# Four half-loaded projections and a new order: a transformer layer on one core

## The chip, the cores and the metric

The kernel runs on one core of a Trainium2 chip. The metric is device time in microseconds (us) of one execution; the median of three runs of the kernel before is 200.46 us (199.8 to 200.73).

## The reference

One layer over 2048 positions of width 512, in bf16: a normalised input goes through a sliding-window attention with 32 heads of 16 (each position sees 8 positions, two apart), the result is added back, normalised again, and goes through a gated feed-forward part of inner width 1376 (1376 = 10 x 128 + 96).

```
h   = x + A(layernorm(x))
  A:  q, k, v = x @ wqkv                          # 512 x 1536
      logits  = q . k[pos - 2*w], w = 0..7, / 4   # masked where pos - 2*w < 0
      o       = softmax(logits) . v[pos - 2*w];  o @ wo
h2  = h + ((relu(hn @ W_gate)) * (hn @ W_up)) @ W_down,  hn = layernorm(h)
```

## The kernel before

The 2048 positions are cut into four chunks of 512 (`tk` 0 to 3; the text writes a step of chunk 2 as `mu1.2`). Everything stays on the chip between load and store. Per chunk the steps are, with the names that the code gives them and the engine that runs them:

- `xst`, `xag` (VectorE statistics), `xrl`, `xre` (ScalarE), `xxn` (VectorE: a normalised row block of 128 positions), then the transpose of the block: on TensorE with an eviction by ScalarE (`xtp` and `xte`; in chunk 0 blocks 1 and 3 are evicted by VectorE, `xtv1`, `xtv3`), or, for all of chunk 3, by four DMA transposes on the SP queue (`xtd`, line 484).
- `qkv0` to `qkv11`: twelve projections of 128 columns (q and k in turn, then four of v), each four TensorE matmuls over the four row pieces of 128 of the weight; ScalarE evicts them (`qe`, line 544). In chunk 0 the first four are cut into halves of 256 positions, `qka0` to `qka3` for the first half and `qkc0` to `qkc3` for the second (lines 547 to 553), so that a half can start when its two row blocks are there.
- `pr1`, `pr0` (VectorE, line 583): products of q with the shifted k, four of 2.2 us per chunk; `sc1`, `sc0` (TensorE, line 589) sum them over each head; `ex` (ScalarE) exponentials; `mk` a mask in chunk 0; `den`, `dl`, `dr` the reciprocal of the denominator; `am` (VectorE) scales the exponentials.
- `bc1`, `bc0` spread the exponentials over a head's partitions (TensorE, evicted as `be`), in chunks 2 and 3 by DMAs on SP (`bd`, line 679). `mu0` to `mu3` (VectorE, line 710) multiply by the shifted v; `tree` sums the eight products. The first addition of a `tree` is in chunks 0 to 2 a DMA that accumulates, `ta` (POOL queue, line 742, 512 KB each).
- `wo0` to `wo3` (TensorE), `rs` (residual), `hnm`, `hsq`, `hrl`, `hre`, `hxn`: second normalisation; its transposes are `htp` and `hte` (TensorE, ScalarE) or DMA transposes `htd` on SP.
- `mm0` to `mm5` (up and gate), `ue`, `ge` (ScalarE), `gu` (VectorE), `dn` (down), `o` (VectorE), `os` (store, on SP but for the last).

The order is fixed at build time. Each step is an `Op` with an engine, a modelled duration and its dependencies; `RANK` gives one number to each of 722 steps, and `Plan.order` (line 116) lets every engine's queue take its own steps in the order of these numbers. Model times only decide in which of several equal buffers a step's result is put. On the chip each engine runs its queue in order, and a step that waits holds up all that stands behind it. The loads are issued ahead of this in `setup` (line 288): four row blocks of x, then the q and k weights in four row pieces of 128 rows, pieces 0 and 2 on the SP queue, 1 and 3 on ACT's (lines 293 and 294), then the second chunk of x and the rest. The planner knows the q and k weights as two loads that land together (`wload["q"]`, `wload["k"]`). `wv_sb` and all later weights follow on SP.

In the first 60 us TensorE takes the projections of all four chunks as filler between the steps that wait for VectorE; then the feed-forward matmuls do that.

The functions that the change touches:

Of the kernel before, what the change touches and what calls it, by code (L numbers as in the profile page):

```python
# [8 lines left out]
P = 128  # L9
# [9 lines left out]
    0, 1, 2, 3, 4, 5, 6, 7, 8, 9, 10, 11, 12, 13, 14, 15, 16, 18, 19, 21,  # L19
    24, 32, 27, 17, 20, 22, 25, 26, 30, 35, 36, 29, 34, 37, 39, 41, 43, 47, 23, 28,  # L20
    31, 33, 38, 45, 48, 42, 59, 65, 40, 51, 55, 46, 56, 60, 49, 52, 57, 73, 76, 61,
    79, 67, 72, 71, 74, 80, 106, 88, 95, 75, 96, 91, 104, 103, 93, 113, 119, 127, 70, 85,
    94, 98, 102, 172, 175, 185, 130, 134, 136, 149, 152, 105, 108, 110, 114, 111, 188, 197, 223, 226,
    231, 179, 190, 217, 221, 228, 171, 180, 208, 211, 219, 158, 169, 195, 207, 210, 245, 252, 236, 241,
    239, 244, 243, 249, 256, 260, 247, 253, 246, 250, 255, 261, 266, 269, 276, 281, 275, 279, 285, 278,
    283, 282, 286, 291, 310, 315, 326, 330, 293, 322, 314, 324, 348, 329, 361, 337, 345, 339, 342, 346,
    350, 365, 333, 358, 349, 354, 340, 352, 353, 356, 363, 323, 328, 316, 321, 302, 313, 308, 312, 332,
    364, 373, 366, 370, 306, 379, 369, 394, 405, 359, 393, 355, 380, 402, 404, 421, 442, 445, 395, 424,
    453, 574, 374, 413, 447, 450, 389, 409, 436, 473, 50, 53, 44, 62, 54, 64, 58, 63, 66, 69,
    77, 90, 78, 83, 92, 81, 87, 82, 86, 89, 118, 129, 157, 170, 124, 196, 164, 178, 97, 101,  # L30
    166, 182, 100, 116, 150, 159, 132, 186, 107, 176, 137, 156, 109, 126, 200, 213, 218, 237, 232, 240,
    251, 258, 262, 264, 274, 284, 287, 288, 296, 294, 292, 298, 300, 307, 305, 309, 303, 318, 327, 360,
    367, 311, 319, 341, 347, 336, 343, 372, 377, 325, 334, 368, 375, 382, 385, 384, 388, 381, 383, 386,
    398, 390, 392, 397, 400, 387, 396, 401, 403, 406, 407, 408, 411, 414, 417, 410, 418, 412, 419, 422,
    457, 467, 434, 484, 477, 480, 461, 481, 491, 472, 475, 429, 466, 449, 460, 441, 476, 478, 433, 435,
    454, 458, 446, 451, 439, 443, 462, 474, 503, 427, 431, 469, 486, 502, 505, 508, 493, 512, 465, 525,
    507, 518, 511, 521, 529, 497, 516, 504, 513, 520, 531, 552, 569, 572, 524, 541, 666, 707, 514, 533,
    537, 540, 536, 539, 580, 708, 112, 120, 99, 121, 68, 84, 115, 122, 125, 133, 144, 163, 147, 160,
    165, 142, 148, 135, 145, 161, 229, 234, 233, 242, 187, 202, 177, 199, 174, 183, 192, 194, 184, 189,
    206, 235, 212, 215, 181, 191, 193, 205, 214, 238, 289, 265, 297, 317, 248, 257, 290, 301, 331, 335,  # L40
    338, 357, 344, 362, 371, 415, 425, 456, 459, 423, 432, 464, 470, 430, 438, 468, 471, 391, 399, 448,
    455, 479, 483, 490, 495, 485, 492, 482, 488, 487, 489, 499, 501, 494, 496, 498, 506, 509, 515, 519,
    522, 526, 528, 527, 534, 517, 532, 596, 601, 562, 594, 565, 589, 558, 591, 604, 544, 553, 542, 551,
    555, 560, 548, 550, 570, 549, 557, 546, 556, 579, 583, 568, 573, 586, 599, 608, 609, 614, 571, 576,
    603, 611, 618, 617, 626, 613, 629, 588, 631, 606, 627, 632, 620, 624, 585, 616, 635, 639, 662, 668,
    672, 623, 641, 643, 677, 628, 636, 638, 675, 634, 637, 645, 647, 117, 141, 128, 139, 131, 140, 123,
    138, 143, 146, 155, 162, 153, 167, 168, 173, 151, 154, 204, 225, 254, 268, 273, 299, 259, 270, 209,
    227, 216, 220, 267, 280, 224, 230, 201, 222, 198, 203, 263, 272, 271, 277, 304, 295, 320, 376, 378,
    351, 416, 420, 426, 428, 437, 444, 440, 463, 452, 530, 535, 543, 561, 500, 510, 523, 566, 547, 554,
    564, 567, 538, 545, 559, 563, 593, 597, 575, 578, 577, 581, 582, 587, 600, 602, 590, 598, 584, 595,  # L50
    592, 605, 607, 610, 619, 622, 615, 625, 621, 633, 612, 630, 657, 689, 683, 687, 667, 673, 671, 680,
    692, 640, 656, 658, 660, 648, 654, 650, 661, 664, 676, 679, 644, 652, 678, 682, 655, 663, 684, 649,
    651, 653, 670, 642, 646, 665, 669, 674, 694, 696, 685, 693, 659, 690, 681, 686, 698, 691, 699, 688,
    697, 701, 710, 714, 717, 719, 705, 709, 711, 715, 695, 702, 704, 706, 700, 703, 712, 713, 716, 718,
    720, 721,
# [36 lines left out]
class Plan:  # L92
# [23 lines left out]
    def order(self):  # L116
# [14 lines left out]
        while left:  # L131
# [36 lines left out]
            op.start, op.done = t, t + op.dur + op.lat  # L168
            if op.dq:
                at = max(t + op.dur + op.dq[0], free.get("DQ", 0.0)) + op.dq[1]  # L170
                free["DQ"] = at
                op.done = at + op.lat
            free[op.eng] = t + op.dur
# [18 lines left out]
def kernel(  # L192
# [19 lines left out]
    DIL = 2  # L212
# [3 lines left out]
    PRE = ()  # L216
    NAB = 0
# [127 lines left out]
    DAL = 5.5  # L345
    TDD, TDL = 1.25, 1.5
# [13 lines left out]
    HG = ([[0, 1, 2, 3]],) * 4  # L360

# [12 lines left out]
    def load(t):  # L374
        return add(None, "LD", 0.0, None, lat=t)

    xload = [[load(t) for t in (3.5, 3.7, 4.1, 4.35)]] + [[load(t)] * BPC for t in (9.15, 13.2, 15.4)]
    wload = {n: load(t) for n, t in
             (("q", 7.78), ("k", 7.78), ("v", 10.6), ("o", 17.1), ("u", 20.5), ("g", 24.0), ("d", 28.5))}
# [139 lines left out]
    for tk in range(NCK):  # L519
# [10 lines left out]
        for n, (c, t) in enumerate(seq):  # L530
# [3 lines left out]
            def f_mm(lo=0, hi=CS, c=c, t=t, mm=mm, xnT=xnT):  # L534
                for dt in range(NT):
                    nc.tensor.matmul(mm.t[:, lo:hi], lhsT=wv_sb[:, dt, t:D:NT] if c == 2 else wqk_sb[:, dt, c * D + t:(c + 1) * D:NT],  # L536
                                     rhs=xnT.t[:, dt, lo:hi], start=(dt == 0), stop=(dt == NT - 1))
# [9 lines left out]
            if tk == 0 and n < 4:  # L547

                a = None
                for i, (lo, hi, evs) in enumerate(((0, 2 * P, xev[0:2]), (2 * P, CS, xev[2:]))):  # L550
                    a = add(("qk%s%d" % ("ac"[i], n), tk), "PE", 4 * MM * (hi - lo) / CS + 0.02,
                            lambda f=f_mm, lo=lo, hi=hi: f(lo, hi), evs + [wl, a, fills[-1]], pr - 5, take=[mm],
                            use=[xnT], lat=PEL if i == 1 else 0.0)
            else:
                a = add(("qkv%d" % n, tk), "PE", 4 * MM, f_mm, xev + [wl], pr, take=[mm], use=[xnT], lat=PEL)
# [13 lines left out]
        for hf in range(2):  # L569
            sc, ex = Buf(at_s), Buf(ex_s)  # L570
            scd, prd = [], []
            for t in range(0, NT, 2):
# [13 lines left out]
                def f_sc(t=t, sc=sc, pb=pb):  # L586
                    for u in range(2):
# [5 lines left out]
                a = add(("pr%d" % hf, tk), "DVE", D40, f_pr, [d[k] for k in (t, t + 1) for d in (qd, kd, kp)],  # L593
                        apr, take=[pb], use=[qT], lat=DL)
                prd.append((a, pb, f_sc))
            if (tk, hf) in PRE:
# [72 lines left out]
        for w0 in range(0, W, BCN):  # L669
            hf = w0 // 4  # L670
            if (tk, hf) in BCD:
                for eng, q in (("SP", nc.sync), ("ACT", nc.scalar), ("POOL", nc.gpsimd)):
# [4 lines left out]
                    def f_bd(ws=ws, q=q, w0=w0, ab=ab, ex=exs[hf]):  # L677
                        for w in ws:
# [3 lines left out]
                                   take=[ab], use=[exs[hf]], lat=0.77, dq=(0.75 - 0.5 * (len(ws) - 1), 0.5 * len(ws))))  # L682
# [19 lines left out]
        for t in range(NT):  # L702
# [13 lines left out]
            def f_om(t=t, mt=mt, rc=rc, OT=OT):  # L716
                V.tensor_tensor(out=OT.t[:, t, :], in0=mt.t[:, 0, :], in1=rc.t[:], op=ALU.mult)

            m = add(("mu%d" % t, tk), "DVE", D40, f_mu, abd + [vd[t], kdone.get(("v", tk - 1, t))], tpr,
                    take=[mt], use=[ab], lat=DL)  # L720
# [17 lines left out]
            for n, du in ((4, D20), (2, D10), (1, D2)):  # L738
                f = lambda n=n, mt=mt, f=f_a: f(n, mt)
                if n == 4 and (tk, t) in DACC:  # L740
                    def f_da(mt=mt):
                        nc.gpsimd.dma_start(mt.t[:, 0:4, :], mt.t[:, 4:8, :], accum_op=ALU.add)  # L742

                    m = add(("ta%d" % t, tk), "POOL", 1.0, f_da, [m], tpr, use=[mt], lat=1.1, dq=(0.75, 2.74))
                    continue
                if n == 1 and tk in EARLY:
                    oev[t] = add(("tree%d" % t, tk), "DVE", du, f_al, [m], tpr, take=[OT], use=[mt], lat=DL)
                else:
                    m = add(("tree%d" % t, tk), "DVE", du, f, [m], tpr, use=[mt], lat=0.11)
# [39 lines left out]
        for f0 in range(0, NFT, 2):  # L789
# [3 lines left out]
            for ft in fts:  # L793
# [4 lines left out]
                def f_mm(w_sb, mm, ft=ft, fs=fs, hnT=hnT):  # L798
                    for dt in range(NT):
                        nc.tensor.matmul(mm.t[:fs, :], lhsT=w_sb[:, dt, ft * P: ft * P + fs],  # L800
                                         rhs=hnT.t[:, dt, :], start=(dt == 0), stop=(dt == NT - 1))
# [4 lines left out]
                def f_ge(gm=gm, gr=gr, fs=fs, i=ft - f0):  # L806
                    nc.scalar.activation(out=gr.t[:fs, i, :], in_=gm.t[:fs, :], func=ACT.Relu)  # L807

                a = add(("mm%d" % (f0 // 2), tk), "PE", 4 * MM, lambda f=f_mm, um=um: f(wu_sb, um), hev + [wload["u"]], pr,
                        take=[um], use=[hnT], lat=PEL)  # L810
                b = add(("ue%d" % (f0 // 2), tk), "ACT", A5, f_ue, [a], pr - 200, take=[ub], use=[um], lat=AL)
                c = add(("mm%d" % (f0 // 2), tk), "PE", 4 * MM, lambda f=f_mm, gm=gm: f(wg_sb, gm), hev + [wload["g"]], pr,
                        take=[gm], use=[hnT], lat=PEL)
# [93 lines left out]
```

## Time and profile before

| | |
|---|---|
| median of three runs | 200.46 us (199.8 to 200.73) |
| the profiled execution, its own time | 201.23 us |
| its span in the trace | 199.5 us |
| TensorE (PE) busy | 191.6 us, 96% |
| VectorE (DVE) / ScalarE (ACT) busy | 152.6 us, 77% / 115.0 us, 58% |
| granted TensorE clock | 1.00 in every stretch asked for |

The profiled execution is 1.73 us longer than its span, and 0.8 us longer than the median of the runs; a difference in the trace is therefore taken off the median. Rows of a timeline give start, duration, engine, line and operation, what is written and read, how many instructions were merged, and in brackets how long the engine was idle before and what ended that. Matmul durations overlap, because matmuls are pipelined: the pace is read from the distance of starts. Four matmuls of 512 positions take 0.86 us in the chain that ended last, a matmul of 256 positions 0.108 us, a transpose 0.055 us.

### The profile page before, as it was taken

Reading aid. Unit: us, or ns where it says so; the run is one execution under the profiler, and the core shown is the slowest. Engines: PE = TensorE matmul, PEld = TensorE weight load, DVE = VectorE, ACT = ScalarE, POOL = GpSimd, SP = SyncE. Lnnn points to the kernel's source line nnn. Section 1 sums busy time; section 2 is a strip of 40 time slices with the busy share of each in tenths; the row PEclk is TensorE's granted clock in tenths of the full one; section 3 lists DMA queues with packets and bytes.
Section 4 is the critical chain, followed back from the end, with each engine's and each line's share of the span. In section 5 each row is a group of like instructions: output and inputs, shape, how many; then the busy total and the mean of one; then the engine's idle time right before and its main releaser. Section 6 shows DMA issues by size and latency. Waiting matters only on the chain.

```text
span 199.5 us, 2918 instructions
## 1 busy us (share of the span) xinstructions
PE 191.6 (96%) x1080; PEld 95.7 (48%) x1099; DVE 152.6 (77%) x239; ACT 115.0 (58%) x240; POOL 12.6 (6%) x28
## 2 busy tenths in 40 slices
PE   8599999999999999999999999999999999999994
PEld 8385445554445344444444444444444444444542
DVE  6669999999999999998899859999964423032332
ACT  3455899881999987663844557701439620456500
POOL 4000000330000004100113000000000000000000
PEclk9999999999999999999999999999999999999999
DMA  6959981897000008985269970140010130102022
GB/s 166 327 185 324 412 283 32 156 192 148 3 0 0 3 0 157 190 165 123 39 118 196 208 204 2 26 85 20 3 53 0 26 79 0 31 0 79 0 79 79
DMA packets 19981, 20.92 MB, mean 105 GB/s; under 512 B 8608, under 2 KB 16768, under 8 KB 19968
## 3 DMA queue, kind: packets, MB, share of 16 engines
q1 hardware_dynamic: 17520, 13.60, 23.0%
q0 software_dynamic: 1728, 6.29, 16.8%
q10 hardware_dynamic: 720, 0.85, 1.6%
q8 instruction: 8, 0.13, 0.3%
q14 instruction: 5, 0.04, 0.1%
HBM read 8.42 MB, written 2.10 MB: 53 GB/s over the span
## 4 chain that ended last, share of the span: by engine, by line
PE 91%; DMA 4%; ACT 2%; issue 1%; SPq 1%; DVE 0%
PE bank L800 37%; PE bank L536 21%; PE bank L837 19%; PE bank L762 7%; DMA wqk_sb<-in_A_wqkv_dram 4%; PE bank L589 3%; PE bank L495 2%; ACT big L695 1%; PE bank L639 1%; ACT quad L511 1%; PE bank L765 0%; SPq L292 0%; PE bank L689 0%; ACT quad L544 0%; SPq L294 0%
## 5 line engine op out<-in xcount | busy, mean ns | idle before, releaser
L800 PE MATMUL bank<-quad,wu_sb 128*128 128x512 bf16 (+1 forms) x170 | 42.7, 379 | 0.7 <-ACT quad L511 0.3
L800 PE MATMUL bank<-quad,wg_sb 128*128 128x512 bf16 (+1 forms) x173 | 41.6, 379 | 0.1
L837 PE MATMUL bank<-wd_sb,gT 128*128 128x512 bf16 (+3 forms) x184 | 39.4, 366 | 0.2
L807 ACT ACTIVATE gr<-bank 128x512 bf16<-128x512 f32 (+1 forms) x44 | 25.3, 601 | 23.3 <-PE bank L800 21.8
L804 ACT CAST up_sb<-bank 128x512 bf16<-128x512 f32 (+1 forms) x44 | 25.1, 588 | 23.2 <-PE bank L800 22.4
L710 DVE TENSOR_TENSOR big<-big,vT 128x4096 bf16<-128x4096 bf16 x16 | 36.1, 2290 | 0.8 <-DMA big<-ex 0.6
L583 DVE TENSOR_TENSOR big<-quad,kT 128x4096 bf16<-128x4096 bf16 x16 | 36.2, 2288 | 0.4 <-ACT quad L544 0.4
L536 PE MATMUL bank<-quad,wqk_sb 128*128 128x512 bf16 (+1 forms) x140 | 30.3, 356 | 2.1 <-DMA wqk_sb<-in_A_wqkv_dram 1.8
L820 DVE TENSOR_TENSOR gT<-gr,up_sb 128x1024 bf16<-128x1024 bf16 (+1 forms) x24 | 15.2, 646 | 20.5 <-ACT up_sb L804 10.4
L837 PEld LDWEIGHTS <-gT 128*128 128x128 bf16 (+1 forms) x187 | 18.2, 98 | 19.7
L800 PEld LDWEIGHTS <-wu_sb 128*128 128x128 bf16 (+1 forms) x176 | 17.5, 100 | 21.1 <-issue 1.3
L800 PEld LDWEIGHTS <-wg_sb 128*128 128x128 bf16 (+1 forms) x176 | 17.6, 100 | 20.5 <-issue 0.2
L536 PEld LDWEIGHTS <-wqk_sb 128*128 128x128 bf16 x144 | 15.5, 114 | 14.3 <-DMA wqk_sb<-in_A_wqkv_dram 2.3
L848 DVE TENSOR_TENSOR row<-x_sm,bank 128x512 bf16<-128x512 bf16 (+1 forms) x17 | 10.8, 653 | 10.6 <-PE bank L837 10.6
L713 DVE TENSOR_TENSOR big<-big 128x1024 bf16<-128x1024 bf16 (+2 forms) x24 | 17.2, 735 | 0.7 <-DMA big<-big 0.6
L742 POOL DMA_DIRECT2D big<-big x12 | 10.5, 872 | 86.8 <-DVE big L710 42.7
L536 PE MATMUL bank<-quad,wv_sb 128*128 128x512 bf16 x62 | 15.2, 380 | 0.1
L762 PE MATMUL bank<-wo_sb,quad 128*128 128x512 bf16 x63 | 15.2, 379 | 0.1
L466 DVE TENSOR_SCALAR row<-x_sm,mv,rs 128x512 bf16<-128x512 bf16 x32 | 11.6, 407 | 2.3 <-ACT rs L448 2.1
L431 DVE BATCH_NORM_STATS2 st<-x_sm 128x6 f32<-128x512 bf16 x16 | 10.5, 680 | 3.4 <-DMA x_sm<-in_A_x_dram 3.4
L420 ACT ACTIVATE row<-x_sm,mv 128x512 bf16<-128x512 bf16 x12 | 8.6, 723 | 5.0 <-DVE mv L412 5.0
L544 ACT CAST kT<-bank 128x512 bf16<-128x512 f32 x16 | 9.2, 592 | 3.4 <-PE bank L536 3.4
(68 smaller groups left out, 141.6 us busy)
## 6 DMA issues: line engine op xcount, KB each, us to landing
big<-big POOLq DMA_DIRECT2D x12, 512.0 KB, 5.5
big<-ex SPq DMA_DIRECT2D x16, 128.0 KB, 2.8
out_dram<-row SPq DMA_DIRECT2D x15, 128.0 KB, 1.8
x_sm<-in_A_x_dram SPq DMA_DIRECT2D x3, 512.0 KB, 6.4
wu_sb<-in_B_W_up_dram SPq DMA_DIRECT2D x1, 1376.0 KB, 9.7
wg_sb<-in_B_W_gate_dram SPq DMA_DIRECT2D x1, 1376.0 KB, 12.7
wd_sb<-in_B_W_down_dram SPq DMA_DIRECT2D x1, 1280.0 KB, 15.7
wqk_sb<-in_A_wqkv_dram ACTq DMA_DIRECT2D x2, 256.0 KB, 7.2
```

The costliest lines, as they stand in the source:

```text
L466: V.tensor_scalar(out=xn.t[:], in0=x, scalar1=mv.t[:, j, 0:1], scalar2=rs.t[:, j:j + 1], op0=ALU.add if residual else ALU.subtract, op1=AL ...
L536: nc.tensor.matmul(mm.t[:, lo:hi], lhsT=wv_sb[:, dt, t:D:NT] if c == 2 else wqk_sb[:, dt, c * D + t:(c + 1) * D:NT], rhs=xnT.t[:, dt, lo:h ...
L583: V.tensor_tensor(out=pb.t[:].rearrange("p (t w) s -> p t w s", t=2), in0=q4, in1=k4, op=ALU.mult)
L710: V.tensor_tensor(out=mt.t[:], in0=ab.t[:], in1=v8, op=ALU.mult)
L713: V.tensor_tensor(out=mt.t[:, 0:n, :], in0=mt.t[:, 0:n, :], in1=mt.t[:, n:2 * n, :], op=ALU.add)
L762: nc.tensor.matmul(od.t[:], lhsT=OT.t[:, t, j * P:(j + 1) * P], rhs=wo_sb[:, t, :], start=(t == 0), stop=(t == NT - 1 and tk not in RPE))
L800: nc.tensor.matmul(mm.t[:fs, :], lhsT=w_sb[:, dt, ft * P: ft * P + fs], rhs=hnT.t[:, dt, :], start=(dt == 0), stop=(dt == NT - 1))
L804: nc.scalar.copy(out=ub.t[:fs, i, :], in_=um.t[:fs, :])
L807: nc.scalar.activation(out=gr.t[:fs, i, :], in_=gm.t[:fs, :], func=ACT.Relu)
L820: V.tensor_tensor(out=gt.t[:fs, 0:n, :], in0=gr.t[:fs, 0:n, :], in1=ub.t[:fs, 0:n, :], op=ALU.mult)
L837: nc.tensor.matmul(od.t[:, c0:c1], lhsT=gts[ft].t[:fs, ft % 2, j * P:(j + 1) * P], rhs=wd_sb[:fs, ft, c0:c1], start=(ft == 0), stop=(ft == ...
L848: V.tensor_tensor(out=ob.t[:, c0:c1], in0=x_sm[:, tk * BPC + j, c0:c1], in1=od.t[:, c0:c1], op=ALU.add)
```

## The change

It has four parts.

1. The first four projections of chunk 0 are cut in three: `qka` and `qkc` are now the two halves of 256 positions over weight row pieces 0 and 1 only, two matmuls each, and a new step `qkd` adds pieces 2 and 3 over all 512 positions, two matmuls. The halves wait for a new planner load `ab` (pieces 0 and 1), `qkd` for the old one. The flag that starts an accumulation is set in the first half only, since both halves now stay open in one PSUM bank until `qkd`.
2. `RANK` is a new list of 727 numbers: four more `qkd` and one more load.
3. The planner's model: later landing times of the loads, and a DMA model in which a transfer from SP or ACT that comes while accumulating DMAs of the POOL queue are under way is slowed (to a share of 0.06 for a DMA transpose, 0.18 for others), and can hold up its queue. This changes planned times, and by them the numbers of the buffers; it issues nothing.
4. Options that are off (`PRD`, `DAC2`, `PRS`, `MUH`, `HSP` are all empty) and the loops that go with them; with them empty the same instructions are issued as before.

```diff
-                for dt in range(NT):
+            def f_mm(lo=0, hi=CS, d0=0, d1=NT, ...):
+                for dt in range(d0, d1):
...
-                                     rhs=xnT.t[:, dt, lo:hi], start=(dt == 0), stop=(dt == NT - 1))
+                                     rhs=xnT.t[:, dt, lo:hi], start=(dt == 0 and lo == 0), stop=(dt == NT - 1))
...
-                a = None
+                ab, done = [wload["ab"]], []
                 for i, (lo, hi, evs) in enumerate(((0, 2 * P, xev[0:2]), (2 * P, CS, xev[2:]))):
-                    a = add(("qk%s%d" % ("ac"[i], n), tk), "PE", 4 * MM * (hi - lo) / CS + 0.02,
-                            lambda f=f_mm, lo=lo, hi=hi: f(lo, hi), evs + [wl, a, fills[-1]], pr - 5, take=[mm],
-                            use=[xnT], lat=PEL if i == 1 else 0.0)
+                    done.append(add(("qk%s%d" % ("ac"[i], n), tk), "PE", 2 * MM * (hi - lo) / CS + 0.005,
+                                    lambda f=f_mm, lo=lo, hi=hi: f(lo, hi, 0, 2), evs + ab + done + [fills[-1]], pr - 5,
+                                    take=[mm], use=[xnT]))
+                a = add(("qkd%d" % n, tk), "PE", 2 * MM, lambda f=f_mm: f(0, CS, 2, NT), done + [wl], pr - 4.9, take=[mm],
+                        use=[xnT], lat=PEL)
...
-    xload = ... for t in (9.15, 13.2, 15.4)]
+    xload = ... for t in (10.8, 14.4, 17.8)]
-             (("q", 7.78), ("k", 7.78), ("v", 10.6), ...
+             (("q", 9.55), ("k", 9.55), ("ab", 8.1), ("v", 12.1), ...
```

The new numbers, set against the list of steps, give the new queues. The places that the prediction speaks of, before and after:

```
TensorE, start
  before: xtp0 xtp1 fill fill | qka1 qka0 xtp2 xtp3 qka2 qka3 | qkc1 qkc3 qkc2 qkc0 | qkv5 qkv6 qkv7 qkv4 qkv10 qkv8
          xtp.1 xtp.1 xtp.1 qkv9 xtp.1 qkv11 | sc1.0
  after:  xtp0 xtp1 fill fill | qka3 qka1 xtp3 xtp2 qka2 qka0 | qkc2 qkc0 qkd0 qkd2 qkc1 qkd1 qkc3 qkd3 |
          qkv6 qkv5 qkv7 qkv4 qkv8 xtp.1 xtp.1 xtp.1 qkv11 xtp.1 qkv10 | sc1.0      (qkv9 stands behind sc0.0 now)
VectorE, start
  before: xxn3 xxn2 | xst.1 xtv3 xst.1 xag xst.1 xst.1 xag xag xag xst.2 | pr1.0 xxn.1 x4 xag.2 pr1.0 pr0.0
  after:  xxn3 xxn2 xtv3 | xst.1 x4 xag.1 x4 | pr1.0 xxn.1 x4 pr1.0 pr0.0           (xst.2 behind pr0.0)
VectorE, chunk 3's rows
  before: xxn.3 xxn.3 xxn.3 mu3.0 xxn.3 mu2.0 mu1.0 mu0.0
  after:  mu3.0 xxn.3 xxn.3 xxn.3 xxn.3 mu2.0 mu1.0 mu0.0
TensorE, before the feed-forward part
  before: ... qkv11.3 qkv2.3 htp.0 x4 bc0.1 sc1.2 mm0.0 sc0.2 bc1.1
  after:  ... qkv11.3 htp.0 x4 qkv9.3 qkv7.3 sc1.2 bc0.1 mm3.0 mm2.0 mm0.0 bc1.1 sc0.2
```

The POOL queue has the same order before and after. On SP the DMAs `bd` of chunk 3 stand ahead of the first four stores. The loads in `setup` are the same.

## The prediction

> **What bounds the kernel now.** I read the page's engine line first, then the chain that ended last.
>
> ```profile
> PE 191.6 (96%) x1080; PEld 95.7 (48%) x1099; DVE 152.6 (77%) x239; ACT 115.0 (58%) x240; POOL 12.6 (6%) x28
> ...
> PE 91%; DMA 4%; ACT 2%; issue 1%; SPq 1%; DVE 0%
> ```
>
> TensorE is busy in nearly all of the span, and the chain runs over it; the other shares are the only places where its order loses time. So the third view is where TensorE stands still: the windows of busy time show full rows from 14 us to the end but for one, and the timeline of TensorE shows the start.
>
> ```profile
> 64.00:70.00 6.00, 5.56 (x65) 2.64 (x65) 6.00 (x8) 5.92 (x11) 0.00 (x0) 1.00 0.01 3
> ```
>
> ```profile
> 8.66 0.41 PE L536 MATMUL bank<-quad,wqk_sb 128*128 128x256 bf16 x2 [0.85 <-DMA wqk_sb<-in_A_wqkv_dram]
> 10.05 0.85 PE L536 MATMUL bank<-quad,wqk_sb 128*128 128x256 bf16 x6 [0.98 <-DMA wqk_sb<-in_A_wqkv_dram]
> 10.73 0.61 PE L495 MATMUL bank<-identity,row 128*128 128x128 bf16 x8
> ```
>
> The second column of the windows row is TensorE's busy time: 0.44 us of 6 are lost. The timeline shows the first projection stop after two matmuls: row pieces 0 and 1 of the weight are there at 8.66, pieces 2 and 3 only at 10.05, and everything else in the queue, the transposes of blocks 2 and 3 included, stands behind that wait. VectorE is the second bound: the windows of 20 to 92 us have it busy all the time but for 0.37 us, so up to there TensorE's lead is worth only what VectorE can follow.
>
> **The change part by part.** *The cut projections.* Work: 32 matmuls of 256 become 16 of 256 and 8 of 512: 32 x 0.108 = 3.46 us against 16 x 0.108 + 8 x 0.216 = 3.46. Eight weight loads less are worth nothing, as they lie beside matmuls. What moves is the waiting. Before, the four projections end at 14.00 (the row of `qkv10` starts at 17.45, less four projections of 0.863). After, from 8.66: `qka3`, `qka1` 0.43 (9.09), eight transposes 0.44 (9.53), `qka2`, `qka0` 0.43 (9.96). Then a wait for the evictions of blocks 2 and 3: the second transpose ends at 9.53, ScalarE's copy starts some 0.2 later (before: transposes from 10.73, copy at 11.15) and takes 0.59, so `qkc2` starts at about 10.37. VectorE's `xtv3` (0.41) is done by then, as its new place is ahead of the statistics. `qkc2`, `qkc0` 0.43 (10.80); pieces 2 and 3 have landed since 10.05; `qkd0`, `qkd2` 0.86 (11.66); the rest 2 x (0.22 + 0.43) = 1.30: the end is 12.96. Gain 1.0 us. Cross-check: between 8.66 and 14.00 TensorE has 3.46 + 0.44 = 3.90 us of work in 5.34, 1.44 idle; 0.4 of it stays.
>
> *VectorE's start.* It waits for x's second chunk until 11.15 whatever happens.
>
> ```profile
> 11.15 0.69 DVE L431 BATCH_NORM_STATS2 st<-x_sm 128x6 f32<-128x512 bf16 x1 [2.80 <-DMA x_sm<-in_A_x_dram]
> 11.76 0.41 DVE L509 COPY quad<-bank 128x512 bf16<-128x512 bf16 x1
> ...
> 14.74 0.69 DVE L431 BATCH_NORM_STATS2 st<-x_sm 128x6 f32<-128x512 bf16 x1 [0.30 <-DMA x_sm<-in_A_x_dram]
> 15.35 2.27 DVE L583 TENSOR_TENSOR big<-quad,kT 128x4096 bf16<-128x4096 bf16 x1
> ```
>
> After, `xtv3` falls into the idle 2.80 (0.33 gained) and the statistic that waited 0.30 for the third chunk stands later: 0.63 gained. The first `pr1.0` starts at 15.35 - 0.63 - 0.62 (the moved statistic) = 14.10; its last input, the fourth projection, is evicted at about 13.8. So TensorE gains 1.0 and VectorE 0.63, and I look where the 0.37 between them must be lost.
>
> *The queues up to 60 us.* At `xtp.1`: the last row is there at 14.10 + 2.21 + 4 x 0.33 = 17.63, TensorE comes to that transpose at 12.96 + 5 x 0.863 + 0.45 = 17.73. At `sc1.0`: the second product ends at 17.63 + 2.21 = 19.84; TensorE, at 21.89 before, has one projection less ahead of it and comes at 21.89 - 0.86 - 1.0 = 20.0. At `wo1.0`: the last product of chunk 0's attention ends at 52.10 - 0.63 = 51.47 (earlier, if the 0.37 of idle time at 43.07 goes), TensorE is there at 53.23 - 0.86 - 1.0 = 51.37. So it is just in time each time: some 0.1 us lost here, 0.2 us over the whole. All of the 0.37 would be the upper end.
>
> *The hole at 64 to 70.* Behind `htp.0` there was no step free of its evictions (`hte`); the new queue has `qkv9.3`, `qkv7.3` and `sc1.2` there, 2 x 0.86 + 0.98 = 2.7 us, over two evictions of 1.0 us each. `hxn.0` comes earlier, since one product (2.2 us) goes behind it: 63.35 - 2.2 - 0.63 = 60.5, and TensorE is at `htp.0` at about 64.25 - 1.73 - 1.0 = 61.5. Gain 0.44.
>
> *After 92 us* VectorE has idle stretches, and the new order only exchanges feed-forward matmuls; TensorE was full there and stays so. The SP queue takes chunk 3's `bd` ahead of four stores; the stores then wait for `am0.3` some 4 us, and their row buffers are wanted by `hsq.2` next. The `os` of chunk 0 land at 4.8 us under load and were issued at 109; the squares start at 119.8, so this hides, and would cost a few tenths without that cover. The end (last `dn`, VectorE 0.42, store) has the same lengths. The option code and the planner's model issue nothing; other buffer numbers could add or remove a wait that no row shows: 0, with 0.3 either way.
>
> *Sum:* 201.23 - 1.0 - 0.44 + 0.2 = 200.0 for the profiled execution, whose time lies 0.77 above the median of the three runs; on the median 200.46 - 1.24 = 199.2 us. Bounds of this case: 1.0 + 0.44 + 0.3 gained (198.7) to 0.63 + 0.2 (199.6), and 0.3 for the buffers: 198.5 to 199.9.
>
> **The rivals.** *(1) Slower: chunk 3's DMA transposes starve.* Before, three of the four `xtd` were done ahead of the first accumulating DMA `ta3.0`. After, `mu3.0` goes ahead of all of chunk 3's rows, so `ta3.0` is issued at about 34.1 (mu3.0 from 31.3; 0.67 from its end to the issue, as before) and the transposes from 34.5 to 38.4, 1.31 us each. What that does is seen on the fourth transpose of before, issued behind `ta3.0`: the DMA view of 37.3 to 40.0 us.
>
> ```profile
> q0 software_dynamic: 128, 0.52, 107.9%
> q1 hardware_dynamic: 103, 0.03, 7.6%
> issues: line engine op xcount, KB each, median us to landing
> big<-big POOLq DMA_DIRECT2D x1, 512.0 KB, 6.0
> quad<-row SPq DMA_TRANSPOSE x1, 5.3
> ```
>
> It got 103 of its 544 packets while the accumulation moved 128 of 144 (1728 over 12), and landed after 5.3 us instead of 2.5. The next stretch shows the rest:
>
> ```profile
> q0 software_dynamic: 42, 0.11, 50.1%
> q1 hardware_dynamic: 441, 0.10, 43.2%
> ```
>
> From 40.0 to 41.2 the other 441 packets went, ahead of most of `ta2.0`, which had been issued at 38.26. If the transposes again go through between two accumulations, all four land when `ta2.0` does at the latest: 38.26 + 6.0 - 0.6 = 43.7. The first projection of chunk 3 stands at 45.1 in the new queue (42.63 before for the first of its chunk, 3.45 later by the work ahead of it, less 1.0). That is the forecast. If instead they get packet for packet until the last accumulation drains (`ta0.0`: 42.39 + 7.0 - 0.6 = 48.8, and half a us more for the rest), TensorE stands still from 45.1 to 49.3 with its whole queue: 199.2 + 4.2 = 203.4. It decides at 45.1; a landing with `ta1.0`, at 40.44 + 6.5 - 0.6 = 46.3, gives 200.4. The Trainium skill, DMA: Bandwidth & Descriptors, section on queues, rings and completion order, says that a DMA engine takes turns between its queues packet by packet. The first of the two rows agrees (103 to 128), the second (441 to 42) only if `ta2.0`'s packets were not yet there; by that rule alone it would be this rival. The second row is the one nearest to the new case, so 0.17.
>
> *(2) VectorE takes it back.* If TensorE waits for VectorE at each of the steps above until it is only 0.63 ahead, and a new hole of the size of the old one (0.44) opens where rows come late, 200.46 - 0.63 = 199.8, and with 0.3 for buffers up to 200.1: no measurable change. For it: margins of 0.1 us. Against: VectorE loses idle time too (0.37 at 43.07), and is not full after 92. 0.20.
>
> *(3) The cut does not do what it says.* If all four row pieces land together at about 10.05, the new queue starts there with 0.43 + 0.44 + 0.43 us of work and then meets the same wait of 0.4: end at 10.05 + 4.30 = 14.35, 0.35 later than before. With the hole closed, 200.46 + 0.35 - 0.44 + 0.2 = 200.6. Against: two separate waits for that DMA in the timeline, 1.39 apart. 0.05.
>
> **How the numbers follow.** The forecast case has 0.58, with its own range 198.5 to 199.9; three quarters of it lie below 199.46, which is 0.5% under the median (1.0 us, about what a measurement of this kernel can tell from no change). Faster: 0.44, and 0.04 from rival 2 and smaller surprises: 0.48. Within 0.5%: 0.14 + 0.16 + 0.05 = 0.35. Slower: rival 1 at 0.17. The range leaves out that rival's far end and little else: 198.4 to 201.4.
>
> **What would show it.** In the trace after: two waits of `qka` gone, the first projection of v (`qkv8`) near 16.4 and not 17.45; the first product at 14.1; a full row from 64 to 70; chunk 3's transposes landing at 39 to 44 and no idle time of TensorE near 45. The forecast is wrong if TensorE has idle time of over 0.5 us anywhere between 13 us and the end, and rival 1 holds if that lies at 45 with the DMA `quad<-row` as its releaser.

## The result and the profile after

The kernel after takes 210.24 us (median of 5 runs, 209.56 to 211.67); before, beside it, 200.46. The ratio is 1.0493, 95% interval 1.0456 to 1.0529: 9.8 us slower, where 1.3 us faster was forecast and 203.4 us was the rival with a chance of 0.17. The profiled execution took 211.67 us, the highest of the runs, with a span of 209.9 us. One execution in what follows is left out of its kernel's time and ratio, because it took over 1.5% longer than the fastest of that kernel: the profiled one of e2_before_rows0.

The page of after, engine line and chain:

```profile
PE 195.8 (93%) x1072; PEld 95.5 (46%) x1091; DVE 152.7 (73%) x239; ACT 116.0 (55%) x240; POOL 12.7 (6%) x28
...
PE 53%; DVE 19%; DMA 13%; ACT 9%; issue 4%; SPq 1%; POOL 0%; DVEq 0%; POOLq 0%; ACTq 0%
```

TensorE held 91% of the chain before; now it holds 53%, and transfers 13%. The chain between 30 and 62 us (start, us, what) names the transfer:

```profile
33.82 4.42 DVE big L758 x2
38.23 0.40 SPq L501
38.64 0.04 issue
38.68 13.02 DMA quad<-row
51.70 0.14 issue
51.84 6.58 PE bank L553 x16
```

Line 501 is chunk 3's DMA transpose `xtd`. The last of the four is issued at 38.68 and lands 13.02 us later. On the POOL queue the second and third accumulation, `ta2.0` and `ta1.0`, are issued on both sides of it:

```profile
36.59 0.86 POOL L801 DMA_DIRECT2D big<-big  x1 [2.68 <-DVE big L758]
38.76 0.86 POOL L801 DMA_DIRECT2D big<-big  x1 [1.31 <-PE bank L553]
```

The first projection of v of chunk 3 waits for the transpose with all of TensorE's queue behind it, as the timeline of TensorE shows:

```profile
40.96 3.40 PE L553 MATMUL bank<-quad,wqk_sb 128*128 128x512 bf16 x15
51.84 1.87 PE L553 MATMUL bank<-quad,wv_sb 128*128 128x512 bf16 x4 [7.48 <-DMA quad<-row]
```

The next 16 matmuls take 6.58 us where four take 0.86 otherwise (16 in 3.45). The windows of after show why; the columns are window and length, busy time (count) of TensorE, its weight loads, VectorE, ScalarE and POOL, then the granted clock, the DMA share and GB/s:

```profile
44.40:47.50 3.10, 0.00 (x0) 0.00 (x0) 2.71 (x4) 1.07 (x2) 0.00 (x0) 1.00 2.37 108
47.50:57.80 10.30, 5.96 (x15) 2.08 (x16) 5.28 (x9) 0.58 (x1) 0.00 (x0) 0.51 0.25 38
57.80:60.00 2.20, 2.20 (x22) 0.83 (x21) 0.00 (x0) 1.54 (x4) 0.00 (x0) 0.98 0.00 0
```

Some 3 us into the wait the granted clock falls to a half and stays there until 57.8, 6 us after the work has come back: 3.1 us more. The wait and the clock are 10.6 us, a little more than the whole loss (9.8 by the medians, 10.4 between the two profiled executions).

The start came out as forecast, even earlier. From the timelines of TensorE and VectorE:

```profile
7.99 0.63 PE L553 MATMUL bank<-quad,wqk_sb 128*128 128x256 bf16 x4
8.45 0.61 PE L512 MATMUL bank<-identity,row 128*128 128x128 bf16 x8
8.90 0.60 PE L553 MATMUL bank<-quad,wqk_sb 128*128 128x256 bf16 x4
9.73 6.21 PE L553 MATMUL bank<-quad,wqk_sb 128*128 128x256 bf16 x31 [0.24 <-ACT quad L528]
15.78 1.03 PE L553 MATMUL bank<-quad,wv_sb 128*128 128x512 bf16 x4
```

```profile
10.65 2.47 DVE L448 BATCH_NORM_STATS2 st<-x_sm 128x6 f32<-128x512 bf16 x4 [1.35 <-DMA x_sm<-in_A_x_dram]
13.16 0.38 DVE L451 BATCH_NORM_AGGREGATE mv<-st 128x2 f32<-128x6 f32 x4
13.45 2.26 DVE L602 TENSOR_TENSOR big<-quad,kT 128x4096 bf16<-128x4096 bf16 x1
```

The cut projections wait 0.24 us in all (1.83 us before), `qkv8` starts at 15.78 (forecast 16.4) and the first product at 13.45 (forecast 14.1). Some of that is luck of this execution: the first weight pieces were there by 7.99 instead of 8.66, x's second chunk at 10.65 instead of 11.15.

What holds the transposes shows in the DMA view, packets of both queues (q0 the accumulations, q1 the transposes; packets, MB, share of the 16 engines, which adds up the packets' times and can pass 100%), first for 40 to 42 us, then for 46 to 48:

```profile
q0 software_dynamic: 72, 0.25, 86.8%
q1 hardware_dynamic: 301, 0.07, 20.0%
...
big<-big POOLq DMA_DIRECT2D x1, 512.0 KB, 12.4
quad<-row SPq DMA_TRANSPOSE x1, 13.0
```

```profile
DMA packets 39, 0.09 MB, mean 47 GB/s; under 512 B 17, under 2 KB 17, under 8 KB 39
...
q0 software_dynamic: 22, 0.09, 184.3%
q1 hardware_dynamic: 17, 0.00, 35.6%
```

Until 46 both queues progress side by side. Then for more than 4 us almost nothing moves: 39 packets in 2 us, of both kinds. An accumulation's packet took 0.39 us of one engine at 40 to 42 (86.8% of 16 engines and 2 us, over 72) and takes 2.7 us now (184.3%, over 22). The last transpose lands at 51.70; the last accumulation `ta0.0`, issued at 40.72, lands 1.4 us later still (12.4 us from issue, instead of 5.7 to 7.3 for the four of e1_rows3).

### The profile page after: what moved, and what is told of

Same layout as the page of the kernel before. It is cut to its first block, busy times and chain, and to the rows that moved or that the text cites. A ratio compares the mean times of both kernels' runs of the same rounds, so it can differ in the third digit from the quotient of the medians.

```text
span 209.9 us, 2922 instructions
## 1 busy us (share of the span) xinstructions
PE 195.8 (93%) x1072; PEld 95.5 (46%) x1091; DVE 152.7 (73%) x239; ACT 116.0 (55%) x240; POOL 12.7 (6%) x28
## 4 chain that ended last, share of the span: by engine, by line
PE 53%; DVE 19%; DMA 13%; ACT 9%; issue 4%; SPq 1%; POOL 0%; DVEq 0%; POOLq 0%; ACTq 0%
PE bank L865 22%; PE bank L910 14%; PE bank L553 11%; DVE big L758 8%; DMA quad<-row 6%; DMA big<-big 4%; PE bank L827 4%; DVE big L602 4%; DMA wqk_sb<-in_A_wqkv_dram 3%; PE bank L608 2%; ACT big L743 2%; DVE gT L893 2%; ACT quad L528 2%; DVE big L761 1%; DVE row L483 1%
## 5 line engine op out<-in xcount | busy, mean ns | idle before, releaser
L865 PE MATMUL bank<-quad,wu_sb 128*128 128x512 bf16 (+1 forms) x173 | 42.6, 379 | 0.7 <-DMA quad<-row 0.5
L872 ACT ACTIVATE gr<-bank 128x512 bf16<-128x512 f32 (+1 forms) x44 | 25.8, 606 | 25.9 <-PE bank L865 21.8
L553 PE MATMUL bank<-quad,wqk_sb 128*128 128x512 bf16 (+1 forms) x132 | 32.3, 387 | 0.5 <-ACT quad L528 0.2
L893 DVE TENSOR_TENSOR gT<-gr,up_sb 128x1024 bf16<-128x1024 bf16 (+1 forms) x24 | 15.0, 641 | 18.7 <-ACT gr L872 12.6
L553 PE MATMUL bank<-quad,wv_sb 128*128 128x512 bf16 x62 | 16.7, 395 | 7.6 <-DMA quad<-row 7.5
L561 ACT CAST quad<-bank 128x512 bf16<-128x512 f32 x16 | 9.1, 596 | 15.4 <-PE bank L553 13.9
L553 PEld LDWEIGHTS <-wv_sb 128*128 128x128 bf16 x64 | 6.9, 115 | 14.1 <-issue 9.3
```

What stands on the lines that cost most here:

```text
L865: nc.tensor.matmul(mm.t[:fs, lo:hi], lhsT=w_sb[:, dt, ft * P: ft * P + fs], rhs=hnT.t[:, dt, lo:hi], start=(dt == 0), stop=(dt == NT - 1))
L893: V.tensor_tensor(out=gt.t[:fs, 0:n, :], in0=gr.t[:fs, 0:n, :], in1=ub.t[:fs, 0:n, :], op=ALU.mult)
```

## The experiments

Two theories stood at first. *The moved rows:* the loss is rival 1, `mu3.0` ahead of all of chunk 3's rows, which puts the transposes behind the first accumulation `ta3.0`. *The rest of the order:* the loss, or much of it, is elsewhere in the new numbers. "Order" edits below permute the numbers of `RANK` for the named steps alone, ahead of the loop in `Plan.order`; buffer numbers may change with them.

**One moved step, both ways.** e1_rows3 is the kernel after with three of chunk 3's rows ahead of `mu3.0` again; e2_before_rows0 is the kernel before with `mu3.0` ahead of all four, and nothing else.

```diff
+        mu = [o for o in self.ops if o.key == ("mu3", 0)]
+        xs = sorted([o for o in self.ops if o.key == ("xxn", 3)], key=lambda o: o.prio)
+        want = xs[:3] + mu + xs[3:]              # e2: xs[:0] + mu + xs
+        for o, p in zip(want, sorted(o.prio for o in want)):
+            o.prio = p
```

> The changed kernel with one thing put back: three of chunk 3's four row blocks (xxn.3) stand ahead of mu3.0 on VectorE again, so three DMA transposes are issued ahead of the first accumulating DMA. Theory S (the transposes starve behind the accumulations, and all else follows from it): TensorE's wait of 7.5 us at the first projection of chunk 3 goes, the granted clock is 1.00 throughout, and the time is 198.7 to 199.9 us. Rival N (the new order is too tight in many places, and the transposes are only one of them): 203 us or more, with idle TensorE after 60 us as in the changed kernel. Rival C (the transposes land late wherever they stand, because of SP's queue): 209 to 211.

> The kernel before with only that step moved: mu3.0 ahead of all four row blocks of chunk 3 on VectorE, nothing else. Theory S: the four transposes share the queues with the accumulations, land 10 us or more after the last is issued, TensorE waits some 7 us at the first projection of chunk 3 (42.6 us before) and loses its clock: 207 to 212 us. Rival N: within 0.5% of 200.5, since one step's place is no search. Rival C: no change either.

e1_rows3: 201.98 us, ratio to before 1.0069 (1.0047 to 1.0092). The wait of 7.5 us is gone and the transposes land after 2.9 us in the median. e2_before_rows0: 211.9 us, ratio 1.0558 (1.052 to 1.0597); its profiled execution took 214.19 us, and TensorE stands in it as in the kernel after, only longer:

```profile
53.45 3.57 PE L541 MATMUL bank<-quad,wv_sb 128*128 128x512 bf16 x8 [10.83 <-DMA quad<-row]
```

Taken back, this one step returns 8.3 of the 9.8 us; made alone, it costs 11.2. But e1_rows3 is still 1.4 us slower than before, 2 us above the upper end of what the forecast's own sum gave for it: something else failed too.

**The clock.** e3_after_fill is the kernel after with 34 matmuls of 512 positions, whose result is overwritten, ahead of the waiting projection.

```diff
+                if tk == 3 and n == 8:
+                    for _ in range(34):
+                        nc.tensor.matmul(mm.t[:], lhsT=identity[:], rhs=wo_sb[:, 0, :], start=True, stop=True)
```

> The changed kernel with 34 matmuls of 512 positions, whose result is thrown away, ahead of the first projection of chunk 3: 34 x 0.216 = 7.3 us of work that waits for nothing, in the place where TensorE stood still. If the drop of the granted clock after the wait (0.61 in the 10 us from 50 us, 16 matmuls in 6.6 us instead of 3.5) costs time of its own, the clock stays at 1.00 and the time falls by about 3 us to 207; if that drop is only a sign of the wait, the time stays at 210.2; if the wait is shorter than 7.3 us in most runs, it is longer than 210.

208.61 us (ratio 1.0403, 1.0372 to 1.0434). The clock stays full, and the projections go on at the usual pace:

```profile
44.37 7.50 PE L554 MATMUL bank<-wo_sb,identity 128*128 128x512 bf16 x34
51.71 1.03 PE L556 MATMUL bank<-quad,wv_sb 128*128 128x512 bf16 x4
```

By the medians the clock is worth 1.6 us, by the two profiled executions (211.67 and 208.37) 3.3. In these two the projections go on at the same time (51.84 and 51.71), so 3.3 is nearly all the clock. The fill has a fixed length and costs something itself where the transpose lands early: in the profiled execution the transpose landed at 50.7 (issued at 38.58, 12.1 to landing), and the projections stood behind the fill until 51.71. So 1.6 is a lower end. It also fits that the other four executions of the kernel after have a mean granted clock of 0.984, where the profiled one has 0.976: half speed for some 6.7 us instead of 10.1 (an estimate from these means and the spans).

**How many transposes, how many accumulations.** What is it that lets transposes through in one order and not in another? e9_rows2 and e10_rows1 put two rows and one ahead of `mu3.0`.

> The kernel after with two rows of chunk 3 ahead of mu3.0, so that two of the four DMA transposes are issued behind the first accumulation ta3.0 (one in e1_rows3 and in the kernel before, four in the kernel after). Theory 'they get through between two accumulations as long as they are few': the later of the two lands some 5 to 6 us after issue, at 42 to 43, TensorE waits less than 0.5 us near 45, time 201.5 to 203. Rival 'whatever stands behind ta3.0 waits until the last accumulation ta0.0 has drained': landing over 10 us after issue, TensorE waits 4 us or more near 45, time 206 or more.

> The kernel after with one row of chunk 3 ahead of mu3.0: three DMA transposes are issued behind ta3.0. Theory 'each transpose behind the first accumulation lets one accumulation more get ahead': the last one lands 8 to 10 us after issue, TensorE waits 2 to 4 us near 45, time 204 to 207. Rival 'all or nothing': as in the kernel after, 13 us and a wait of 7 us, 210 to 212; or no wait at all, as with one transpose, 201.5 to 203.

They took 212.88 and 213.19 us, with waits of 8.61 and 8.54: worse than the kernel after. But they did not put two and three transposes behind `ta3.0`, as was meant. SP's queue takes the rows in an order of its own, and its first transpose waited for a row behind `mu3.0`; the four were issued from 34.72 and 34.85 on, with `ta3.0` at 34.95 and 34.48, and ended later than in the kernel after. e13_rows2_sp and e14_rows1_sp let SP's order follow VectorE's; e15_three_accumulations and e8_two_accumulations are the kernel after, with one or two of chunk 0's accumulations as additions on VectorE.

```diff
+        xt = [o for o in self.ops if o.key == ("xtd", 3)]          # e13, e14
+        for o, p in zip(sorted(xt, key=lambda o: min(xs.index(d) for d in o.deps if d in xs)), sorted(o.prio for o in xt)):
+            o.prio = p
...
+    DACC = tuple(x for x in DACC if x != (0, 0))                   # e15; e8: x not in ((0, 0), (0, 1))
```

> This is the kernel after, but the last two of chunk 0's four accumulating DMAs (ta1.0 and ta0.0) are additions on VectorE again, some 1.2 us each; ta3.0 and ta2.0 stay, so all four transposes of chunk 3 are still issued behind the first accumulation. Theory 'starved until the last accumulation has drained': ta2.0 is issued at about 36.6 and drains by 42 to 43, the transposes land by 43.5, TensorE's wait of 7.5 us falls below 0.5, and with VectorE's 2.4 us more the time is 202 to 204. Rival 'any mixing clogs both queues for its own time': landing of the last transpose still over 8 us after issue, a wait of TensorE of over 3 us.

> In e9_rows2 and e10_rows1 SP's queue takes the rows in another order than VectorE makes them, so SP's first transpose waited for a row behind mu3.0 and all four were again issued with or behind ta3.0 (34.7 us and later). Here SP's order follows VectorE's: two rows and two transposes ahead of ta3.0, two behind. Theory 'it goes by how many transposes are left when the accumulations follow each other': as in e1_rows3, the last lands 5 to 6 us after issue, no wait of TensorE near 45, time 201.5 to 203. Rival 'one behind is the limit': a wait of 4 us or more, time 206 or more.

> The same with one row ahead of mu3.0: one transpose is issued ahead of ta3.0 and three behind. Theory 'it goes by how many are left': three are on the wrong side of the limit between two and four or on the right one; by the packets that e9_rows2 moved in the gaps (some 350 of 544 per accumulation) the last one is through by 44 to 45, with ta1.0: a wait of 0 to 1.5 us, 202 to 204. Rival 'all or nothing': a landing of over 10 us, a wait of 6 us or more, 208 or more.

> The kernel after, with only the last of chunk 0's accumulating DMAs (ta0.0) turned into an addition on VectorE; four transposes behind ta3.0. In e8 (without ta1.0 and ta0.0) the last transpose landed 6.1 us after issue, in the kernel after 13.0, and there both queues hardly moved from 46 to 50.5. Theory 'each accumulation holds the transposes up for its own time': landing of the last transpose 8 to 9 us, at 46.5 to 47.5, TensorE waits 2 to 3 us, 204 to 206. Rival 'the long packets from 46 on come only with the fourth accumulation and the last transposes in it': landing under 7 us, no wait over 1 us, 202 to 203.5.

| kernel | accumulations in chunk 0 | of these issued ahead of the last transpose | last transpose issued at, us | issue to landing, us | wait of TensorE, us | time, us |
|---|---|---|---|---|---|---|
| before | 4 | 1 | 36.20 | 5.3 | 0 | 200.46 |
| e13_rows2_sp | 4 | 1 | 36.43 | 5.1 | 0 | 202.04 |
| e14_rows1_sp | 4 | 1 | 37.75 | 6.7 | 0.31 | 201.8 |
| e1_rows3 | 4 | 1 | 36.62 | 5.2 | 0 | 201.98 |
| after | 4 | 2 | 38.68 | 13.0 | 7.48 | 210.24 |
| e2_before_rows0 | 4 | 2 | 40.77 | 12.5 | 10.83 | 211.9 |
| e9_rows2 | 4 | 3 | 40.24 | 12.7 | 8.61 | 212.88 |
| e10_rows1 | 4 | 3 | 40.37 | 12.6 | 8.54 | 213.19 |
| e15_three_accumulations | 3 | 2 | 38.52 | 7.9 | 2.31 | 205.56 |
| e8_two_accumulations | 2 | 2 | 38.63 | 5.3 | 0 | 202.66 |

(e8, e9, e10, e13, e14 and e15 are single runs; issue, landing and wait are those of the profiled execution, for e2 the one of 214.19 us. The 6.1 us that the expectation of e15 gives for e8 is its third transpose.) e13 had one transpose behind `ta3.0` and not two as expected, because the third row follows `mu3.0` faster than the accumulation is issued. It is not the number of transposes behind `ta3.0` that parts the rows of the table: e14 and e9 have three each. With four accumulations they part by the second, `ta2.0`: with the last transpose issued ahead of it the landing takes 5 to 7 us, behind it 12.5 to 13. In e14 it is ahead by only 0.05 us, so the place of the limit is no more than what these eight rows have in common. With the fourth accumulation taken out (e15) the transpose behind `ta2.0` lands at 46.4, with two taken out at 43.9. So the accumulations hold it, and the last one costs by far the most. In the kernel after 2099 of the transposes' 2176 packets had gone by 46.0 (the windows of two us from 36 on: 612, 492, 301, 278, 416): the stop of the DMA view holds the last 77. It stands in e2, e9 and e10 too (27 to 44 packets in a window of two us), and in none of the other kernels of the table.

SP's queue adds a little. The issue of a transpose itself takes longer beside an accumulation, and the next one stands behind it; two rows of SP's timeline of after, each one instruction:

```profile
33.52 1.36 SPq L501 DMA_TRANSPOSE quad<-row  x1
```

```profile
34.94 2.39 SPq L501 DMA_TRANSPOSE quad<-row  x1
```

At the forecast's 1.31 us each the last would have been issued at 37.45 instead of 38.68, still behind `ta2.0` (36.59).

What a landing with the third accumulation costs, e15's timeline of TensorE and its windows show:

```profile
46.56 1.03 PE L554 MATMUL bank<-quad,wv_sb 128*128 128x512 bf16 x4 [2.31 <-DMA quad<-row]
```

```profile
46.00:47.50 1.50, 0.94 (x5) 0.56 (x6) 1.50 (x1) 0.00 (x0) 0.00 (x0) 1.00 0.00 0
47.50:50.50 3.00, 3.00 (x9) 1.08 (x8) 3.00 (x7) 0.00 (x0) 0.00 (x0) 0.53 0.00 0
```

After a wait of 2.31 us the clock was halved too: the 16 matmuls behind it take 5.32 us, 1.9 more than at full clock (3.45).

**What the rest of the order is worth.** In e1_rows3 TensorE waits where nothing stood before (its timeline):

```profile
51.49 1.04 PE L832 MATMUL bank<-wo_sb,quad 128*128 128x512 bf16 x4 [0.59 <-DVE quad L770]
60.23 0.38 PE L691 MATMUL bank<-ex,same 128*128 128x512 bf16 x1 [0.34 <-ACT ex L671]
62.58 1.07 PE L517 MATMUL bank<-identity,row 128*128 128x128 bf16 x16 [0.25 <-DVE row L488]
104.59 1.89 PE L870 MATMUL bank<-quad,wu_sb 128*128 128x512 bf16 x8 [0.45 <-DMA quad<-row]
```

The first three lie in 50 to 70 us, where its windows lose 1.41 us (0.54 before); the last is `htd.1`, again transposes beside an accumulation (`ta3.2`), 4.9 us from issue to landing. Two edits go at these waits on top of e1_rows3: e5_cover moves the last three rows of chunk 2 behind `xag.3` on VectorE, where it waited 1.22 us, and `dr.0` behind `xre.3` on ScalarE; e6_cover_mu32 also moves `mu3.2` behind `hxn.1`. (`behind` gives steps the numbers right after that of a named step.)

```diff
+        behind(step("xxn", 2)[1:], step("xag", 3)[-1].prio)
+        behind(step("dr", 0), step("xre", 3)[0].prio)
+        behind(step("mu3", 2), step("hxn", 1)[-1].prio)            # e6 only
```

> This is e1_rows3 with two more moves: VectorE's last three rows of chunk 2 stand behind the xag.3 of chunk 3, where they cover the wait for ScalarE's rs, and ScalarE's dr.0 stands behind xre.3. In e1_rows3 VectorE stood still 1.22 us there, and TensorE then waited 0.59 us at wo1.0, 0.34 at den.1 and 0.25 at htp.0. Theory 'margins' (what e1_rows3 still lost, it lost because the queues are just in time): VectorE gets about 1.2 us back, these waits of TensorE shrink to 0.3 us together at most, time 201.98 - 0.9 = 201.1 us, 200.8 to 201.4. Rival 'other buffers or pace': the waits move elsewhere or the time stays within 0.3 us of 201.98.

> As e5_cover, and mu3.2 stands behind the four hxn.1 rows on VectorE, so that the two DMA transposes htd.1 are issued ahead of the accumulation ta3.2. In e1_rows3 they landed 4.9 us after issue and TensorE stood still 0.45 us. Theory: the transposes land after some 3 us, the wait of 0.45 at 104 is gone, time 0.3 to 0.6 us below e5_cover. Rival: VectorE waits for ScalarE's rs ahead of hxn.1 instead (some 1 us of mu3.2 no longer covers it), TensorE's wait comes back at the matmuls that need hxn.1: same as e5_cover within 0.2.

e5_cover: 201.69 us (ratio 1.0052, 1.0036 to 1.0068), 0.3 below e1_rows3 instead of 0.9. The wait at `wo1.0` fell from 0.59 to 0.24, and the one at `den.1` rose from 0.34 to 0.52: handed on. VectorE itself still waits 0.99 us where it was to be covered (1.22 in e1_rows3). e6_cover_mu32: 203.12 us (ratio 1.0131, 1.0108 to 1.0154). The wait for `htd.1` is gone, as expected, but VectorE now waits 2.11 us for ScalarE's `rs`, `mu3.2` follows later, and TensorE pays 0.74 at 101.7 and 1.33 at 117.4. The rival's mechanism was right, its price was not: it said the same as e5_cover within 0.2, and it is 1.4 more.

**What the cut is worth.** e4_before_cut is the kernel before with the cut projections and `xtv3` ahead of the statistics. e7_before_shift adds two moves of the new order: the statistic and aggregate of chunk 2 that stood ahead of the first product go behind `pr0.0`, and `qkv2.3` goes behind `htp.0`. e12_shift_no_cut has these two moves without the cut.

```diff
+        behind(step("xst", 2)[:1] + step("xag", 2)[:1], step("pr0", 0)[0].prio)     # e7, e12
+        behind(step("qkv2", 3), step("htp", 0)[-1].prio)
```

> The kernel before with only the cut of the first four projections (and xtv3 ahead of the statistics of chunk 1, without which the second halves start no earlier): the order of everything else as before. The prediction's step: the four projections end 1.0 us earlier, and TensorE keeps that where VectorE follows: 199.4 us if all of it, 199.8 if VectorE's 0.3 to 0.6 is the limit. Rival: filler and VectorE's steps are in the old order, so the lead is waited away before 60 us: 200.4 us, no change.

> This is e4_before_cut (order of before, cut projections, xtv3 earlier) with two more moves out of the new order: the statistic and aggregate of chunk 2 that stand ahead of the first product go behind pr0.0, and the projection qkv2.3 goes behind htp.0. Theory 'VectorE's start': the first product starts at 13.5 to 13.9 and not at 15.18, TensorE's waits for rows at 18.16 and 18.80 (0.60 and 0.25) go, the hole at 64 to 70 (0.44) closes: 200.67 - 0.85 - 0.44 = 199.4 us, 199.0 to 200.0. Rival 'handed back': VectorE loses the lead again further on (it does the moved statistic 0.7 us later and waits for ScalarE or the loads there), TensorE waits at another step: 200.3 to 200.8.

> The kernel before with the statistic and aggregate of chunk 2 behind pr0.0 and qkv2.3 behind htp.0, as in e7_before_shift (199.85 us), but without the cut of the first four projections and with xtv3 in its old place. Theory 'the cut is needed for the early product': the first product waits for the last of the four projections and starts at 14.2 to 14.7 instead of 13.35, half of e7's gain or more is lost: 200.2 to 200.8 us. Rival 'the cut is worth nothing': first product at 13.4 to 13.8, time within 0.2 us of e7, 199.7 to 200.1.

| kernel | time, us | ratio to before | first product starts |
|---|---|---|---|
| e4: cut alone | 200.67 | 1.0006 (0.9989 to 1.0023) | 15.18 |
| e12: moves alone | 200.69 | 1.0018 (0.9989 to 1.0047) | 14.45 |
| e7: cut and moves | 199.85 | 0.9963 (0.9947 to 0.9979) | 13.35 |

Each alone is worth nothing that the runs can tell, both together 0.8 us. VectorE's timeline says why, for e4, e12 and e7 in turn:

```profile
14.57 0.69 DVE L439 BATCH_NORM_STATS2 st<-x_sm 128x6 f32<-128x512 bf16 x1 [1.43 <-DMA x_sm<-in_A_x_dram]
15.18 2.27 DVE L593 TENSOR_TENSOR big<-quad,kT 128x4096 bf16<-128x4096 bf16 x1
```

```profile
14.45 2.29 DVE L589 TENSOR_TENSOR big<-quad,kT 128x4096 bf16<-128x4096 bf16 x1 [0.61 <-ACT quad L550]
```

```profile
13.07 0.37 DVE L448 BATCH_NORM_AGGREGATE mv<-st 128x2 f32<-128x6 f32 x3
13.35 2.26 DVE L599 TENSOR_TENSOR big<-quad,kT 128x4096 bf16<-128x4096 bf16 x1
```

With the cut alone the first product stands behind a statistic that waits for x's third chunk, and TensorE, 1.8 us early (15.67 against 17.45), waits at 18.16 and 18.80 for the rows behind that product (0.60 and 0.25). With the moves alone the product waits for the uncut projections. e7_before_shift needs both and beats the two kernels that were compared: 0.37% below before. Its 64 to 70 is full (5.95 of 6), but 60 to 64 loses 0.31.

## Why the prediction was wrong

*The step that failed* is the choice between the two readings of one row. The forecast held that four transposes go through between accumulations as one had (441 packets against 42 in 40.0 to 41.2 us), landing by 43.7; packet for packet until the accumulations drain was rival 1. For the first three, the forecast was right: they landed 5.1 to 5.8 us after issue. The fourth came at 38.68, behind `ta2.0` and just ahead of `ta1.0` at 38.76. With the first three gone (1632 packets), 467 of its 544 packets had moved by 46.0, beside the accumulations and not in a gap between them, and the last 77 met the stop: it landed at 51.7. One gap, seen for one transfer, was used for four in a row. e15_three_accumulations lands the fourth at 46.4, 0.4 after its last accumulation, `ta1.0`, has landed: that is the middle case of the prediction ("with `ta1.0`"). That its 46.3 agrees is luck, since `ta1.0` was issued 1.8 us earlier than assumed (38.62) and took 7.4 us instead of 5.9. The fourth accumulation makes it 51.7, past the 49.3 of rival 1.

*Rival 1* named the place (45.1; measured 44.36), the releaser and the step. Its price was too small in three terms. The wait was 7.48 us instead of 4.2, because the transfers did not share the engines to the end but stopped. And it had no term for the clock: 3.1 us in the chain, 1.6 us or more by e3_after_fill. The third is the 199.2 that it starts from: without the stall the new order takes 201.98 (e1_rows3). The three are more than the whole difference, because a TensorE that is late no longer meets every wait of e1_rows3. In e15 the missing clock term (1.9) is nearly as large as the wait itself (2.31). So the middle case, priced at 200.4, measured 205.56; 2.8 us of the difference are the 199.2 again, and e15 has one addition more on VectorE.

*Slips of the working,* which do not change the forecast: the accumulations were kept at their old times, but followed `mu3.0` and were issued 1.7 us earlier (`ta2.0` at 36.59 and not 38.26). The 0.6 us that is taken off each landing has no row behind it: `ta1.0` and `ta0.0`, issued at 38.76 and 40.72, land by the view after 10.0 and 12.4 us, at 48.76 and 53.12, and VectorE's waits for them end at 48.80 and 53.10. And VectorE was idle for 0.56 us between 20 and 92 before (71.44 busy of 72), not 0.37.

The Trainium skill (DMA: Bandwidth & Descriptors, section on queues, rings and completion order), which the prediction weighed, lets a DMA engine switch between queues packet by packet. It pointed to the right side, but the packets that the profile counts follow no fixed turn: 72 to 301 at 40 to 42 us, 22 to 17 at 46 to 48, with the engines counted as busy. Whether one packet of the profile is one turn, no run shows. By itself the rule gave neither the limit at `ta2.0` nor the stop.

*(a) The cut* removed the waits that it was to remove. Forecast 1.0 us. Measured, with `xtv3` moved ahead as well, e7 against e12: 0.84 by their times, 1.1 by their ratios, each to a kernel before that ran beside it (0.4 to 1.8, an estimate from their intervals). What the forecast did not say is that this hangs on the moved statistic: without it the cut gives nothing (e4).

*(b) VectorE's start* was right: the first product starts 1.9 us earlier than before, where 1.25 was forecast, part of it by earlier loads.

*(c) The margins* of 0.1 us up to 60 us were the second failure. The sum had 0.2 us lost there; the order without the stall (e1_rows3, e13, e14) waits 0.32 to 0.59 at `wo1.0` and 0.34 to 0.45 at `den.1`, and is 1.4 us slower than before. *(d) The hole* at 64 to 70 closed (5.88 of 6 in e1_rows3), but 0.34 and 0.25 opened at 60 and 62. *(e) "After 92 us nothing"* was wrong by 0.45: `htd.1` beside `ta3.2`. Rival 2's words (margins lost, a new hole) describe e1_rows3 well, but its 199.8 was 2 us short. The starts in the timelines account for the whole: from its first projection of v (15.80, before 17.45) to its last row of `dn` (187.67, before 186.81) TensorE takes 2.5 us longer in e1_rows3. By the distance of starts the four waits are 0.78, 0.50, 0.40 and 0.63 (the figure in brackets counts from a modelled end and is some 0.17 short), and stops at 69.3, 98.7 and 115.8 add 0.35, 0.32 and 0.17: 3.2 us, where before has 0.6. What each single wait is worth is argued; e5 and e6 show only that single edits hand the waits on.

*What stays open:* why both queues nearly stop in the last 77 packets. The runs show when (the last transpose issued behind the second of four accumulations), not what holds the packets. Counts and times change together in these edits, so whether the limit is one of number, of order or of time is not settled.

## What to carry to other kernels

Before a step is moved on one engine, list the transfers that it releases and those it delays, on every queue, and look at which now overlap; here one multiplication moved ahead of four transposes cost 11.2 us. A wait of TensorE of some two us or more (2.31 was the shortest seen to do it) has to be priced with the clock that it loses afterwards, not with its length alone. And a gain on one engine counts only together with what frees the engine behind it: the cut and the moved statistic were worth nothing apart and 0.8 us together.

## What the runs showed of the hardware

- Four DMA transposes of 128 x 512 beside four accumulating transfers of 512 KB: the last transpose 13.0 us from issue to landing, 2.5 alone, with 39 packets moved in 2 us; and SP's issue of a transpose up to 3.02 us (the one at 38.68) instead of 1.2 to 1.3.
- The granted clock fell to 0.5 some 3 us after TensorE's work stopped and came back 6 us after it resumed (after: 47.6 to 57.9). In e15 it fell at 47.6, 1 us after a wait of 2.31 us had already ended, and stayed low for 3.4 us. Neither delay is fixed: in e2_before_rows0 the clock fell 5 us after the work had stopped (47.6, after 42.6) and came back 4.4 us after it resumed (57.8, after 53.45). It was low for 10.2 us there, as in the kernel after, e9 and e10, whether the wait was 7.48 or 10.83 us. The Trainium skill (TensorE: Matmul & The Clock Gate, section on HAM oscillation) advises no idle gaps over some 3.4 us; the measured limit here is lower: a wait of 1.33 us left the clock full (e6, 1.00 from 116 to 124), and one of 2.31 us did not.
- Loads issued alike landed 0.7 us or more apart between executions (TensorE waited for the first weight pieces until 8.66 before and 8.29 in e13, and had them by 7.99 in the kernel after), which is as much as the cut is worth: a gap of the start in one profile is not its mean.
